# Group 0's root mean square as columns spread by a product, and its last two units normalised on ScalarE

## The chip, the cores and the metric

The kernel runs on one core of a Trainium2 chip. The metric is the device time of one execution in microseconds (us); lower is better. Instructions are carried out by TensorE (PE; its weight loads are shown as PEld), VectorE (DVE), ScalarE (ACT) and GpSimd (POOL), each in the order of its own queue; SyncE (SP) issues the transfers.

## The reference

Causal attention over 4 batches, 12 heads, 448 positions and a head width of 64, then a gated feed-forward layer on the 1792 tokens (model width 768, inner width 1536) with an RMS normalisation ahead of it:

```python
scores = np.where(mask, -1e9, q @ k.T / sqrt(64))
attn = softmax(scores)                      # sum + 1e-9 in the denominator
x = (attn @ v)  -> (1792, 768)
rms = np.sqrt(np.mean(x * x, axis=-1, keepdims=True) + 1e-06)
xn = x / rms * rms_g
g = xn @ w_gate
out = (g * sigmoid(g) * (xn @ w_val)) @ w_out
```

The weights come in as 64-bit numbers; the kernel turns them into 32-bit ones by integer steps.

## The kernel before

Attention is cut into 60 units (two heads and a block of queries each), in three groups: units 0 to 11 are group 0, 12 to 23 group 1, the rest group 2. A pair of units of group 0 makes one chunk `xr[0, c]` of 128 features by 512 tokens; there are six chunks, c = 0 to 5, and units 10 and 11 make the last one. A unit goes through scores (L192), mask and maximum (L201, VectorE), exponentials (L204, ScalarE), the reciprocal of the row sums (L213) and the multiplication with it (L207 on ScalarE for group 1, L209 on GpSimd for the others), transposes on TensorE (L249) with a copy of each half to `pt` (L253 VectorE, L255 ScalarE), products with the values (L275), and a copy to `xr` (L290).

Of each chunk `square` (L297) takes the squares; for group 0 GpSimd does this and the running sum `acc` for chunks 0 to 4 (both are shown as L103), and VectorE the square of chunk 5 (L308). `split_x` makes a rounded part `xh` (L328, ScalarE) and the rest `xl` (L329, VectorE). `rms` (L333) sums the squares over the features by products with a matrix of ones, so that each of the 128 rows of the result holds all 512 sums (L337), takes the root on ScalarE (L339) and four reciprocals of 128x128 on VectorE (L342). The result, `rinv[0]`, is multiplied into the first products by `evict` (L457).

The feed-forward layer walks over 36 weight chunks s (each 128x768) for a group. In the first pass a chunk is loaded (L360), converted (L379 ScalarE, L380 GpSimd, L382 and L384 VectorE), written back for later passes (L386), and split into `w_h` (L394, ScalarE) and `w_l` (L396, VectorE). Of `w_h` and `w_l` there are four buffers each, so that the cast of chunk 4 waits for TensorE's last use of chunk 0. Products are in triples (L440, L441, L442), six triples to a chunk; in what follows one triple is a part. The parts of weight chunks 0 to 2 with the chunks c of group 0 that are ready are done early, between the last units. The gate's products go through L457, a Tanh (L458), L459; the value's are multiplied in by L467; the product of both is rounded (L468) and its rest taken (L470).

The order of the work is written out by hand: a list of steps is walked, a slot number `now` goes up by one after each, and `post(delay, fn)` puts work into the slot `delay` later. Delays stand in the table `T`. Around the end of group 0 the slots are: 67 and 73 the multiplications of units 10 and 11; 75 the square and sum of chunk 4; 85 the products of unit 11; 87 the square of chunk 5, then the last part of token chunk 3; 88 `rms`; 88 to 90 the three parts of token chunk 4; 93 the conversion of weight chunk 5 (`CONVERT`, L47); from 94 the main loop with the parts of token chunk 5; 97 the cast of weight chunk 4; 98 the first `evict`.

```python
            if ENDS[0] <= p < ENDS[1]:
                pr["norms"].append(lambda: nc.scalar.mul(sp, sp, rs))
```

`ENDS` is (12, 24, 60), so p there is a unit of group 1. A later function, `x_steps` (L491), does for group 2 what the change does for group 0: sums as columns (L501), root (L503), reciprocal (L504), diagonal blocks (L510 on ScalarE, L512 on GpSimd), and a product that spreads them (L517).

Of the kernel before, what the change touches and what calls it, by code (L numbers as in the profile page):

```python
# [10 lines left out]
F32 = mybir.dt.float32  # L11
# [9 lines left out]
DM = H * D  # L21
# [17 lines left out]
        for g in range(NG) for c in range(NP)}  # L39
# [2 lines left out]


T = dict(c0=0, c1=1, c2=4, c20=12, c3=4, c30=13, c26=6, c36=7, c5=6, c50=16, c56=9, exp=1, exp0=3, gt=1, hh=1, hl=4, ws=5, ld2=7,
         ld=4, ld1=11, lv=5, norm0=7, norm1=2, r0=1, r1=5, so=3, wl=2, wl0=7, wl2=5, wl4=0, xl=2, xl0=9)
LOAD = (4, 12, 24, 36, 48, 60, 74, 86)
CONVERT = (20, 32, 44, 56, 62, 93)  # L47
SPLIT = (33, 45, 57, 70)
# [14 lines left out]
def attention_ffn(ctx: ExitStack, tc: tile.TileContext, qk0, qk1, qk2, v, v2, w, g, out, out2):  # L63
# [30 lines left out]
    def bank(tag, bufs=1):  # L94


        return ps.tile([P, W], F32, tag=tag, name=tag + "_ps", bufs=bufs)
# [23 lines left out]
    eps = const.tile([P, 1], F32, name="eps")  # L121
    nc.vector.memset(eps, 1e-6)
    tiny = const.tile([P, 1], F32, name="tiny")
    nc.vector.memset(tiny, 1e-9)
    g_sb = const.tile([P, KD], F32, name="g_sb")

# [4 lines left out]
    def post(delay, fn):  # L131
        if delay <= 0:
            fn()
        else:
            later.setdefault(now[0] + delay, []).append(fn)
# [36 lines left out]
    def steps_s(p):  # L172
# [22 lines left out]
        def softmax(e, i, pss):  # L195
            o, wd = bl[i]
            ps, sp = pss[e][:, o: o + wd], pr["sp"][e][:, o: o + wd]
            n = len(bl) * e + i
            nm, sm, rs = (pr[m][:, n: n + 1] for m in ("nm", "sm", "rs"))
            mk = mask2 if kind == 2 else mask[:, 3 * P - wd:]  # L200
            nc.vector.tensor_tensor_reduce(  # L201
                out=sp, in0=ps, in1=mk, scale=nsc, scalar=3.0e38,
                op0=ALU.add, op1=ALU.min, accum_out=nm)
            post(T["exp" if p >= ENDS[0] else "exp0"], lambda: nc.scalar.activation(  # L204
                sp, sp, AF.Exp, bias=nm, scale=-1.0, accum_out=sm))
            if ENDS[0] <= p < ENDS[1]:
                pr["norms"].append(lambda: nc.scalar.mul(sp, sp, rs))  # L207
            else:
                pr["norms"].append(lambda: nc.gpsimd.tensor_scalar(  # L209
                    sp, sp, rs, 1.0, op0=ALU.mult, op1=ALU.mult))  # L210
# [48 lines left out]
    def steps_a(p):  # L259


        if not 0 <= p < len(UNITS):
            return []
        g_, kind, c, k, _, base = UNITS[p]
        pr = hs[p]
        kb, nq = KB[kind], QUERIES[kind]

        def products():
            for h in range(1 + (kind == 2)):
                at = 0  # L270
                for j in range(NKB[kind]):
                    q0, n = ((0, 2 * P), (P, P))[j] if kind == 0 else (D * h, (P, D)[kind - 1])
                    a0 = at + (D * h if kind == 2 else 0)
                    for e in (0, 1):
                        nc.tensor.matmul(  # L275
                            av_ps[e * D: (e + 1) * D, p % 2, q0: q0 + n], raw_v[p][:kb, h, j, e, :],
                            pr["pt", e][:kb, a0: a0 + n], start=(j == 0), stop=(j == NKB[kind] - 1))
                    at += n if kind == 0 else P

        def copy():  # L280
            if g_ == 2 and base == 0:
                if c < 3:
                    xq[c] = w64_p.tile([P, 2, XT], F32, tag="w64", name="xq")
                xr[g_, c] = xq[c % 3][:, c // 3]
            elif base == 0:
                xr[g_, c] = xr_p.tile([P, W], F32, tag="xr", name="xr")
            x = xr[g_, c][:, base: base + nq]
            if p == LAST[g_, c]:
                post(2, lambda: square(g_, c))
            (nc.scalar.copy if g_ == 1 else nc.vector.tensor_copy)(x, av_ps[:, p % 2, :nq])  # L290

        return [products, copy]
# [4 lines left out]
    def square(b, c):  # L297

        halves = [(0, HX), (HX, XT)] if b == 2 else [(0, W)]
        for j, (lo, hi) in enumerate(halves):  # L300
            x = xr[b, c][:, lo: hi]
            sq = rm_p.tile([P, W], F32, tag="sq", name="sq") if c else \
                rm_p.tile([P, W], F32, tag="acc", name="acc", bufs=2)
            sq = sq[:, : hi - lo]
            if b:
                nc.scalar.activation(sq, x, AF.Square)
            elif c == NP - 1:
                nc.vector.tensor_tensor(sq, x, x, op=ALU.mult)  # L308
            else:
                pool_op(sq, x, ALU.mult, x)  # L310
            if c == 0:
                acc[b, j] = sq
            elif b or c < NP - 1:
                pool_op(acc[b, j], acc[b, j], ALU.add, sq)
        if b == 2:
            return
        if c == NP - 1:
            post(T["r1" if b else "r0"], lambda: rms(b, [acc[b, 0]] if b else [acc[b, 0], sq]))
        waiting.append((b, c))

    def split_x():
        if not waiting:
# [6 lines left out]
        post(T["xl0" if b == 0 and c < NP - 1 else "xl"], lambda: nc.vector.scalar_tensor_tensor(  # L329
            out=l, in0=x, scalar=gc, in1=f32(h), op0=ALU.mult, op1=ALU.subtract))  # L330
        xh[b, c], xl[b, c] = h, l

    def rms(b, parts):  # L333

# [688 lines left out]
```

## Time and profile before

| | us |
|---|---|
| median of 3 runs | 692.46 |
| lowest, highest | 692.16, 692.47 |
| the profiled execution | 691.53 |
| its span, first to last instruction | 689.8 |
| TensorE busy in the span | 669.2 (97%) |
| VectorE busy | 537.5 (78%) |
| ScalarE busy | 375.2 (54%) |
| GpSimd busy | 312.3 (45%) |

TensorE's granted clock was 1.000 of full speed over the span. The shares are means over stages with different limits; the wait that ends last in a stage tells more. In a timeline each line gives the start and the duration in us, the engine, the line of the kernel, the operation, output and inputs, and how many such instructions the line sums up; a bracket at its end tells how long the engine stood idle before it and what ended that. An instruction's duration can include time in which it stood at the head of its engine, unable to go on.

### The profile page before, as it was taken

What the parts mean: (1) busy time and instruction counts of PE and PEld (TensorE: products, weight loads), DVE (VectorE), ACT (ScalarE), POOL (GpSimd) and SP (SyncE); (2) the same over time, 40 slices, a digit from 0 to 9 for tenths busy, and PEclk for the clock granted to TensorE, in tenths of its full rate; (3) what the DMA queues carried; (4) which work ended last, traced back from release to release, by engine and by line L of the source; (5) the groups of instructions that cost most, each with busy time, mean ns of one, the idle gap of its engine ahead of it and who ended that gap; (6) DMA issues with size and microseconds to landing.
All of it is one profiled execution on the core that took longest, in us unless ns stands there. A gap on an engine that the chain in (4) does not pass through costs nothing. (4 is left out here: it accounts for less than half of the span.)

```text
span 689.8 us, 11922 instructions
## 1 busy us (share of the span) xinstructions
PE 669.2 (97%) x4108; PEld 548.8 (80%) x4108; DVE 537.5 (78%) x1048; ACT 375.2 (54%) x844; POOL 312.3 (45%) x281
## 2 busy tenths in 40 slices
PE   9889989999999999999999999999999999999997
PEld 6556767777776767777877777888999999999997
DVE  4996989899988577777686968389386768679993
ACT  6974577887887446345364544434434342455550
POOL 4994212131225533747666566663363536312220
PEclk9999999999999999999999999999999999999999
DMA  8663778788879646575757555324667576552541
GB/s 268 220 217 128 229 240 271 217 264 264 261 225 341 228 120 222 184 253 181 262 172 272 178 198 180 126 89 153 191 206 246 181 244 214 184 168 74 173 140 66
DMA packets 71356, 138.80 MB, mean 201 GB/s; under 512 B 7744, under 2 KB 39232, under 8 KB 71296
## 3 DMA queue, kind: packets, MB, share of 16 engines
q1 hardware_dynamic: 71296, 138.05, 62.1%
q8 instruction: 32, 0.52, 0.3%
q14 instruction: 28, 0.23, 0.1%
HBM read 104.21 MB, written 33.82 MB: 200 GB/s over the span
## 5 line engine op out<-in xcount | busy, mean ns | idle before, releaser
L209 POOL TENSOR_SCALAR sp<-sp,rs 128x128 f32<-128x128 f32 (+2 forms) x120 | 82.2, 704 | 89.5 <-DVE rs L213 84.7
L440 PE MATMUL m_ps<-xh,w_h 128*128 128x512 f32 x276 | 117.6, 426 | 4.0 <-DVE t_sb L467 3.0
L204 ACT ACTIVATE sp<-sp,nm 128x384 f32<-128x384 f32 (+3 forms) x168 | 87.1, 521 | 39.7 <-DVE nm L201 39.7
L442 PE MATMUL m_ps<-xh,w_l 128*128 128x512 f32 x276 | 108.5, 393 | 0.0
L441 PE MATMUL m_ps<-xl,w_h 128*128 128x512 f32 x276 | 108.2, 392 | 0.0
L380 POOL TENSOR_SCALAR w<-w 128x768 f32<-128x768 f32 x36 | 40.1, 1113 | 101.6 <-ACT w_c L379 93.5
L103 POOL TENSOR_TENSOR a_l<-w_q,a_h 128x768 fp32r<-128x768 f32 x24 | 47.1, 1964 | 66.6 <-ACT a_h L481 66.5
L275 PEld LDWEIGHTS a_ps<-pt,v_r 128*64 128x64 f32 (+1 forms) x864 | 41.7, 137 | 35.8 <-DVE pt L253 10.3
L275 PE MATMUL a_ps<-pt,v_r 128*64 128x128 f32 (+2 forms) x864 | 60.6, 268 | 7.6 <-DVE pt L253 5.6
L440 PEld LDWEIGHTS m_ps<-xh,w_h 128*128 128x128 f32 x276 | 51.9, 188 | 16.9 <-issue 7.5
L103 POOL TENSOR_TENSOR w_l<-w_r,w_h 128x768 fp32r<-128x768 f32 x30 | 59.5, 1990 | 7.3 <-ACT w_h L394 7.1
L442 PEld LDWEIGHTS m_ps<-xh,w_l 128*128 128x128 f32 x276 | 51.8, 188 | 11.8
L253 DVE COPY pt<-t_ps 128x384 f32<-128x384 f32 (+1 forms) x71 | 42.4, 598 | 23.7 <-PE t_ps L249 23.3
L201 DVE CUSTOM_DVE_ANT_0 sp<-s_ps,mask 128x128 f32<-128x128 f32 (+3 forms) x136 | 49.7, 414 | 12.2 <-PE s_ps L192 11.2
L440 PE MATMUL m_ps<-hh,w_h 128*128 128x512 f32 x144 | 58.6, 407 | 0.0
L441 PEld LDWEIGHTS m_ps<-xl,w_h 128*128 128x128 f32 x276 | 52.2, 189 | 7.8 <-issue 0.2
L442 PE MATMUL m_ps<-hh,w_l 128*128 128x512 f32 x144 | 56.3, 391 | 0.0
L441 PE MATMUL m_ps<-hl,w_h 128*128 128x512 f32 x144 | 56.2, 390 | 0.0
L249 PE MATMUL t_ps<-ident,sp 128*128 128x128 f32 (+1 forms) x309 | 50.3, 275 | 0.4 <-POOL sp L209 0.2
L249 PEld LDWEIGHTS t_ps<-ident,sp 128*128 128x128 f32 (+1 forms) x309 | 38.0, 138 | 14.9 <-POOL sp L209 2.2
L396 DVE TENSOR_TENSOR w_l<-w_c,w_h 128x768 fp32r<-128x768 f32 x36 | 40.1, 1114 | 4.3 <-ACT w_h L394 4.3
L384 DVE SCALAR_TENSOR_TENSOR w_c<-w_c,w 128x768 int32<-128x768 int32 x36 | 41.5, 1153 | 2.0
(185 smaller groups left out, 1677.8 us busy)
## 6 DMA issues: line engine op xcount, KB each, us to landing
w<-in_w SPq DMA_DIRECT2D x36, 768.0 KB, 5.2
w<-w_c SPq DMA_DIRECT2D x36, 384.0 KB, 5.8
w_r<-w SPq DMA_DIRECT2D x36, 384.0 KB, 4.8
qk_r<-in_qk SPq DMA_DIRECT2D x48, 256.0 KB, 4.2
qk_r<-in_qk SPq DMA_DIRECT2D x12, 512.0 KB, 5.7
v_r<-in_v SPq DMA_DIRECT2D x12, 448.0 KB, 4.7
v_r<-in_v SPq DMA_DIRECT2D x24, 192.0 KB, 3.1
wy<-w_r SPq DMA_DIRECT2D x24, 192.0 KB, 4.8
```

Of the source, the lines that this page charges most:

```text
L103: nc.gpsimd.tensor_tensor(out_, a, b, op=op)
L201: nc.vector.tensor_tensor_reduce(out=sp, in0=ps, in1=mk, scale=nsc, scalar=3.0e38, op0=ALU.add, op1=ALU.min, accum_out=nm)
L204: post(T["exp" if p >= ENDS[0] else "exp0"], lambda: nc.scalar.activation(sp, sp, AF.Exp, bias=nm, scale=-1.0, accum_out=sm))
L209: pr["norms"].append(lambda: nc.gpsimd.tensor_scalar(sp, sp, rs, 1.0, op0=ALU.mult, op1=ALU.mult))
L249: nc.tensor.transpose(ps[:kb, at: at + P], pr["sp"][e][:, o + kb * j: o + kb * (j + 1)], ident)
L253: nc.vector.tensor_copy(pt[:kb, :at], ps[:kb, :at])
L275: nc.tensor.matmul(av_ps[e * D: (e + 1) * D, p % 2, q0: q0 + n], raw_v[p][:kb, h, j, e, :], pr["pt", e][:kb, a0: a0 + n], start=(j == 0), ...
L380: (T["c1"], lambda: nc.gpsimd.tensor_scalar(hf_, hf_, 0.0, 1.0, op0=ALU.mult, op1=ALU.mult)),
L384: (at3, lambda: nc.vector.scalar_tensor_tensor(out=ti, in0=ti, scalar=3, in1=lo, op0=ALU.logical_shift_left, op1=ALU.bitwise_or)),
L440: nc.tensor.matmul(ps, wh[:, k, :], mh, start=(first and k == ks[0]), stop=False)
L441: nc.tensor.matmul(ps, wh[:, k, :], ml, start=False, stop=False)
L442: nc.tensor.matmul(ps, wl[:, k, :], mh, start=False, stop=(last and k == 5))
```

## The change

In group 0 the sums of squares are taken with the squares as stationary operand and one column of ones, so that the sum of each token lies in a row: four products for the sum of chunks 0 to 4 in slot 87, four for chunk 5 in slot 88. The root is then taken of 128x4 values. In slot 89 VectorE takes their reciprocal and multiplies the unit matrix with each of the four columns, which gives `dg`, 128x512; in slot 91 a product of ones with `dg` spreads the values to all rows, and ScalarE copies the result to `rms`. A root of one column is put into ScalarE's queue in slot 80, so that the table for roots is loaded there. Units 10 and 11 are normalised on ScalarE.

```diff
--- before.py
+++ after.py
@@ -42,7 +42,7 @@
 
 
 T = dict(c0=0, c1=1, c2=4, c20=12, c3=4, c30=13, c26=6, c36=7, c5=6, c50=16, c56=9, exp=1, exp0=3, gt=1, hh=1, hl=4, ws=5, ld2=7,
-         ld=4, ld1=11, lv=5, norm0=7, norm1=2, r0=1, r1=5, so=3, wl=2, wl0=7, wl2=5, wl4=0, xl=2, xl0=9)
+         ld=4, ld1=11, lv=5, norm0=7, norm1=2, r0=1, dg=1, spread=3, r1=5, so=3, wl=2, wl0=7, wl2=5, wl4=0, xl=2, xl0=9)
 LOAD = (4, 12, 24, 36, 48, 60, 74, 86)
 CONVERT = (20, 32, 44, 56, 62, 93)
 SPLIT = (33, 45, 57, 70)
@@ -121,6 +121,7 @@
     eps = const.tile([P, 1], F32, name="eps")
     nc.vector.memset(eps, 1e-6)
     tiny = const.tile([P, 1], F32, name="tiny")
+    warm_up = const.tile([P, 1], F32, name="warm_up")
     nc.vector.memset(tiny, 1e-9)
     g_sb = const.tile([P, KD], F32, name="g_sb")
 
@@ -203,7 +204,7 @@
                 op0=ALU.add, op1=ALU.min, accum_out=nm)
             post(T["exp" if p >= ENDS[0] else "exp0"], lambda: nc.scalar.activation(
                 sp, sp, AF.Exp, bias=nm, scale=-1.0, accum_out=sm))
-            if ENDS[0] <= p < ENDS[1]:
+            if ENDS[0] - 2 <= p < ENDS[1]:
                 pr["norms"].append(lambda: nc.scalar.mul(sp, sp, rs))
             else:
                 pr["norms"].append(lambda: nc.gpsimd.tensor_scalar(
@@ -285,6 +286,8 @@
             elif base == 0:
                 xr[g_, c] = xr_p.tile([P, W], F32, tag="xr", name="xr")
             x = xr[g_, c][:, base: base + nq]
+            if p == ENDS[0] - 2:
+                post(1, lambda: nc.scalar.activation(warm_up, eps, AF.Sqrt))
             if p == LAST[g_, c]:
                 post(2, lambda: square(g_, c))
             (nc.scalar.copy if g_ == 1 else nc.vector.tensor_copy)(x, av_ps[:, p % 2, :nq])
@@ -314,8 +317,11 @@
                 pool_op(acc[b, j], acc[b, j], ALU.add, sq)
         if b == 2:
             return
-        if c == NP - 1:
-            post(T["r1" if b else "r0"], lambda: rms(b, [acc[b, 0]] if b else [acc[b, 0], sq]))
+        if c == NP - 1 and b:
+            post(T["r1"], lambda: rms(b, [acc[b, 0]]))
+        elif c == NP - 1:
+            cols = column_sums(acc[b, 0], None, True)
+            post(T["r0"], lambda: rms_first(column_sums(sq, cols, False)))
         waiting.append((b, c))
 
     def split_x():
@@ -329,6 +335,34 @@
         post(T["xl0" if b == 0 and c < NP - 1 else "xl"], lambda: nc.vector.scalar_tensor_tensor(
             out=l, in0=x, scalar=gc, in1=f32(h), op0=ALU.mult, op1=ALU.subtract))
         xh[b, c], xl[b, c] = h, l
+
+    def column_sums(sq, ps, first):
+
+        ps = bank("t")[:, : W // P] if first else ps
+        for i in range(W // P):
+            nc.tensor.matmul(ps[:, i: i + 1], sq[:, P * i: P * (i + 1)], ones[:, :1],
+                             start=first and i == 0, stop=not first, skip_group_check=True)
+        return ps
+
+    def rms_first(ps):
+
+        rc = st_p.tile([P, W // P], F32, name="rc", bufs=1)
+        dg = ht_p.tile([P, W], F32, tag="t", name="dg")
+        r = rinv[0] = rm_p.tile([P, W], F32, tag="rms", name="rms", bufs=2)
+        nc.scalar.activation(rc, ps, AF.Sqrt, bias=eps, scale=1.0 / DM)
+
+        def diagonal():
+            nc.vector.reciprocal(rc, rc)
+            for i in range(W // P):
+                nc.vector.tensor_scalar_mul(dg[:, P * i: P * (i + 1)], ident, rc[:, i: i + 1])
+
+        def spread():
+            ps = bank("t")
+            nc.tensor.matmul(ps, ones, dg, start=True, stop=True)
+            nc.scalar.copy(r, ps)
+
+        post(T["dg"], diagonal)
+        post(T["spread"], spread)
 
     def rms(b, parts):
```

## Rows read from the trace of the kernel before

**Rows 1.** Stretches: PE, PEld, DVE, ACT, POOL busy (instructions), clock, DMA share, GB/s.

```profile
75.00:100.00 25.00, 20.98 (x100) 15.66 (x100) 23.59 (x49) 16.83 (x42) 4.10 (x4) 1.00 0.86 259
...
110.00:120.00 10.00, 10.00 (x56) 7.65 (x55) 9.88 (x20) 6.76 (x16) 2.27 (x2) 1.00 0.86 281
```

**Rows 2.** Timeline of TensorE: two of its waits for other engines.

```profile
53.99 0.44 PE L249 MATMUL x_ps<-ident,sp 128*128 128x128 f32 x2 [1.05 <-POOL sp L209]
...
88.32 0.47 PE L440 MATMUL m_ps<-xh,w_h 128*128 128x512 f32 x1 [2.08 <-DVE t_sb L467]
```

**Rows 3.** Timeline of VectorE: the four reciprocals and what follows them.

```profile
63.04 3.39 DVE L342 RECIPROCAL rms<-rms 128x128 f32<-128x128 f32 x4 [1.37 <-ACT rms L339]
66.35 0.90 DVE L396 TENSOR_TENSOR w_l<-w_c,w_h 128x768 fp32r<-128x768 f32 x1
```

**Rows 4.** Timeline of ScalarE around the root of group 0.

```profile
60.91 1.28 ACT L339 ACT_TABLE_LOAD   x1
62.32 0.69 ACT L339 ACTIVATE rms<-t_ps,eps 128x512 f32<-128x512 f32 x1
62.91 0.87 ACT L379 ACTIVATE w_c<-w 128x768 f32<-128x768 f32 x1
64.86 0.84 ACT L394 CAST w_h<-w_c 128x768 fp32r<-128x768 f32 x1 [1.08 <-PE m_ps L441]
```

**Rows 5.** Timeline of TensorE: the sums, then parts of token chunks 4 and 5.

```profile
60.40 1.02 PE L337 MATMUL t_ps<-acc,ones 128*128 128x512 f32 x2
...
62.81 0.40 PE L440 MATMUL m_ps<-xh,w_h 128*128 128x512 f32 x1
...
64.20 0.39 PE L440 MATMUL m_ps<-xh,w_h 128*128 128x512 f32 x1
```

**Rows 6.** Timelines of GpSimd, then VectorE, while units 10 and 11 are made.

```profile
46.28 1.87 POOL L103 TENSOR_TENSOR acc<-acc,sq 128x512 f32<-128x512 f32 x1
...
49.69 5.86 POOL L209 TENSOR_SCALAR sp<-sp,rs 128x128 f32<-128x128 f32 x8
...
51.98 1.96 POOL L209 TENSOR_SCALAR sp<-sp,rs 128x256 f32<-128x256 f32 x1
...
55.51 1.04 POOL L103 TENSOR_TENSOR sq<-xr 128x512 f32<-128x512 f32 x1
...
47.06 1.91 DVE L384 SCALAR_TENSOR_TENSOR w_c<-w_c,w 128x768 int32<-128x768 int32 x1
...
51.79 1.01 DVE L384 SCALAR_TENSOR_TENSOR w_c<-w_c,w 128x768 int32<-128x768 int32 x1
52.73 0.94 DVE L396 TENSOR_TENSOR w_l<-w_c,w_h 128x768 fp32r<-128x768 f32 x1
54.47 0.56 DVE L253 COPY pt<-x_ps 128x384 f32<-128x384 f32 x1 [0.79 <-PE x_ps L249]
```

**Rows 7.** Timelines of GpSimd and VectorE: a later running sum beside VectorE.

```profile
217.52 1.97 POOL L103 TENSOR_TENSOR acc<-acc,sq 128x512 f32<-128x512 f32 x1
...
218.28 1.76 DVE L329 SCALAR_TENSOR_TENSOR xl<-xr,g_sb,xh 128x512 fp32r<-128x512 f32 x1
```

**Rows 8.** Timeline of ScalarE: four multiplications of group 1; two copies of group 0.

```profile
86.76 1.49 ACT L207 ACTIVATE sp<-sp,rs 128x128 f32<-128x128 f32 x4 [2.83 <-DVE rs L213]
...
51.48 0.48 ACT L255 COPY pt<-t_ps 128x384 f32<-128x384 f32 x1 [1.65 <-PE t_ps L249]
...
56.46 0.48 ACT L255 COPY pt<-t_ps 128x384 f32<-128x384 f32 x1 [3.87 <-PE t_ps L249]
```

**Rows 9.** Timelines of TensorE, ScalarE, GpSimd: column sums, root and diagonal of group 2.

```profile
438.99 1.39 PE L501 MATMUL t_ps<-ones,acc 128*128 128x1 f32 x12
440.24 0.49 PE L440 MATMUL m_ps<-hh,w_h 128*128 128x512 f32 x1
...
440.42 0.27 ACT L503 ACTIVATE rc<-t_ps,eps 128x6 f32<-128x6 f32 x1 [2.38 <-PE t_ps L501]
...
441.08 1.60 POOL L512 TENSOR_SCALAR dg<-ident,rc 128x128 f32<-128x128 f32 x3 [0.94 <-DVE rc L504]
```

## The prediction

> **What bounds the kernel now.** I read the stretches first, because a share over the whole span hides them. From 110 us TensorE is busy in every microsecond; between 75 and 100 us it works 20.98 of 25 us while VectorE works 23.59 [rows 1]. So the reader is to see two stages: a long one in which only TensorE's own work or a late hand-over counts, and before it a short one, from the end of group 0's attention to about 106 us, in which VectorE is full and TensorE waits for it (the largest of these waits is 2.08 us, for the product of the two halves, L467 [rows 2]). All of this change lies in or just before that short stage. VectorE works its queue in order and stands still nowhere for long between 66.35 us and that wait; its few gaps are round trips of its own results through ScalarE. Hence one number decides: when does VectorE start the queue at the weight remainder `w_l` of chunk 4 (L396)? Before, at 66.35 us, right behind the four reciprocals of 3.39 us that began at 63.04 [rows 3]. Its other input, the cast `w_h`, was started at 64.86 [rows 4] and so done at 65.70; the reciprocals were the later one by 0.65 us. Every tenth by which this start moves, moves the TensorE wait at 88.32 and then the end, since behind 106 us nothing stands open that could take it up.
>
> Second, what comes before: the last two units (10 and 11) are normalised on GpSimd in eight multiplications, 5.86 us from 49.69; the last of unit 10 ended at 53.94, and TensorE waited 1.05 us for it [rows 2, 6].
>
> **The change part by part: the normalisation.** GpSimd loses the eight multiplications. ScalarE does four such in 1.49 us [rows 8], so it gets 2.98 us. Unit 10's are queued ahead of unit 11's exponentials, unit 11's behind the cast of chunk 3; ScalarE had 1.65 us idle before its copy at 51.48 [rows 8] and a little more ahead of that cast, so that copy of unit 10's transposes comes some 0.8 us later, at about 52.4. TensorE's 1.05 us wait goes. If nothing else moved, the next late thing would be VectorE's copy of the other half (L253): it needs VectorE free, which was so at 53.67, behind `w_l` (52.73 plus 0.94), where it now starts at 54.47 [rows 6]. Gain then: 0.8 us.
>
> But GpSimd's queue closes up. The square and the running sum of token chunk 4 stood behind the eight multiplications and ran at 55.51, when VectorE had little to do [rows 6]. With GpSimd free from 49.69 the square waits only for `xr`, whose copy stands in VectorE's queue right ahead of the conversion of chunk 4, and so it lands in that conversion: a first step (L382) that ends at about 51.7, just ahead of L384, then L384, then L396. These two engines shut each other out: the sum at 46.28 took 1.87 us, and L384 at 47.06, issued behind it, took 1.91 and ended 0.82 us after the sum did [rows 6]. So: square from 51.7, 1.04 us alone [rows 6] less 0.17 of start-up, to 52.6; L384 to 53.4; then the sum, issued at 52.6, 1.1 us (47.06 to 48.15 [rows 6]) to 54.5; L396 0.82 more, to 55.3; and only then the copy, 0.8 us later than before. TensorE's products of unit 10, and everything of group 0's end behind them, come 0.8 us late in place of 0.8 us early. I take this sum.
>
> Does the sum or L396 come first at 53.4? Two rows differ. The sum issued at 217.52 went ahead of a VectorE operation issued at 218.28, which ended 0.55 us after it [rows 7]; but the multiplication issued at 51.98 ended only at 53.94, behind L396, which was issued later, at 52.73, and ran its undisturbed 0.94 us [rows 6]. That multiplication carries a per-token factor and the sum does not, so I go by rows 7. The Trainium skill, page "SBUF — State Buffer", section "Who interferes with whom", has one rule for it: "Issue order, not op shape, decides who blocks". By that rule the sum goes first, as in my forecast; the multiplication at 51.98 doesn't follow it, and by that row the result would be the second rival below.
>
> **The table load.** It took 1.28 us at 60.91 and was over by 62.32, when the last product came in [rows 4], so moving it saves nothing by itself. It moves ahead of ScalarE's copy of unit 11's transposes, before which ScalarE had 3.87 us idle [rows 8]: hidden there. Without that cover the new, shorter chain would show up to 1.3 us of it.
>
> **The sums on TensorE.** Removed: four passes of 512 columns, from 60.40 to 62.81 less one part (one triple of products, 0.69 us: 62.81 to 64.20 is two), so 1.72 us [rows 5]. Added: eight products of one column, two instructions each; twelve such instructions took 1.25 us, 438.99 to 440.24 [rows 9], so two lots of eight are 1.67 us; and the spread, half of what was removed, 0.86 us. In all 0.8 us more on TensorE, of which the first lot stands ahead of the part of chunk 3 and the spread behind the three parts of chunk 4. The spread thus starts at 60.40 + 0.8 (late) + 1.67 + 2.08 = 64.95. Its operand: the columns are in at about 62.9, the square root is 0.27 us [rows 9], the reciprocal of four columns less, and four multiplications of 128x128 on VectorE, which the trace doesn't show. On ScalarE one is 0.37 us at most (a mean with wider ones [rows 8]), on GpSimd 0.53 [rows 9]: with the first they end at 64.9, just in time; with the second 0.6 us late, which TensorE would wait. Anything cheaper changes nothing. I take no wait, the first row being nearer to VectorE's kind, and keep 0.6 for the upper end. `dg` takes one of four rotating `t` buffers and gives it back before the second evict needs it: nothing.
>
> **The reciprocals and the copy.** VectorE is rid of 3.39 us [rows 3] and gets some 1.5. That would be the gain, but what is late next takes it. The spread's result is copied to `rms` on ScalarE, and this copy is put into its queue at slot 91. Behind it there stand the conversion of chunk 5 (L379, slot 93) and the cast `w_h` of chunk 4 (L394, slot 97); before, they ran at 62.91 and 64.86, the second waiting for TensorE alone [rows 4]. Now both wait behind a copy that waits for the spread. Two instructions of the old product ran 1.02 us to the end of the second [rows 5]: the spread ends at 65.97, the copy starts at 66.0, takes 0.6 (62.32 to 62.91 of the square root, as wide [rows 4]), L379 0.8 to 0.87, L394 0.84 [rows 4]: the cast is done at 68.25. VectorE waits for it with `w_l`, and behind `w_l` stand the first gate product and all of the full stage. Start at 68.25 in place of 66.35: 1.9 us later. VectorE's saving of 1.9 us turns into idle time ahead of it.
>
> **The sum.** +1.9 us, carried to the end. The profiled execution, 691.53 us (its span of 689.8 and 1.73 around it, which stay), becomes 693.4; the median of the runs is 0.93 above the profiled execution, so 692.46 + 1.9 = 694.4 us. Differences under about 0.2% (1.4 us) can't be told from none here.
>
> **Rivals.** (a) *GpSimd does not get in the way*: the square and the sum lose to VectorE each time. Then group 0 ends 0.8 us early, the spread starts at 63.35, the cast is done at 66.65: +0.3, 692.8 us, not slower by anything measurable. It is decided at the end of the conversion before L384: against it, 47.06 [rows 6]. Chance 0.1. (b) *Half of it*: the square goes ahead of L384, the sum behind L396, as the multiplication at 51.98 did. The copy then starts at 54.2, 0.3 early; spread at 63.85, cast at 67.15: +0.8, 693.3 us. Chance 0.2. (c) *The saved VectorE time arrives*: ScalarE's queue is not the bound, either because the copy comes early enough or because the casts stand ahead of it. Then the first cast is bound by the part of chunk 0 behind the spread, which frees its buffer; with (a) that is 63.35 + 0.86 + 0.65, cast done at 65.7: -0.65, 691.8 us; more would need the full stage itself to close up, for which I see one sort of reason, other encounters of GpSimd and VectorE behind 66 us. Against it: the slots, by which the copy precedes both. Chance 0.12, half of it faster by more than 0.2%. (d) *The operand of the spread is late* by 0.6: 695.0 us, chance 0.15. The forecast as it stands has 0.43.
>
> **How the numbers follow.** Slower by more than 0.2% (over 693.85 us): the forecast and (d), and a little of (b), 0.62. Within 0.2%: (a), most of (b), half of (c), 0.32. Faster: 0.06. The range reaches down past (a) to 692.2, and up past (d) to 695.3; the forecast's own range is 693.9 to 694.9.
>
> **What would show it.** Right: GpSimd's square near 51 us with some 1.7 us and its sum to about 54.5; L384 and L396 of that place stretched to 1.6 and 2.0 us; the copy L253 at 55.2; the spread at about 64.9 with no wait; ScalarE's copy near 66, then L379 and L394 without a pause; VectorE idle up to a `w_l` at 68.2; TensorE's waits of 1.05 and 2.08 us still there, 1.9 us later. Wrong: the copy L253 at 53.7 to 54.2 (rivals a, b), a `w_l` before 66.4 (c), a wait of TensorE at the spread for VectorE (d). If the late start shows but the TensorE wait at 88 us shrinks by as much, my claim that nothing behind takes it up was wrong.

## The result, and the profile after

The changed kernel takes 700.36 us (median of 4 runs, 699.13 to 700.65), the kernel before 692.31 beside it (4 runs, 690.93 to 692.47): a ratio of 1.0117, with a 95% interval from 1.0100 to 1.0135. It is 8.05 us slower; 694.4 was forecast, and the upper end of the range was 695.3. The profiled execution of after took 700.35 us, with a span of 698.6 against 689.8.

Laying VectorE's rows of the two traces side by side shows where the 8.8 us come in. After is 0.64 late from its first softmax on (the first load landed that much later; this differs from one execution to the next and is not the change's). It is 2.47 late at `w_l` of chunk 4, 2.4 to 2.9 late all through the long stage up to 490 us, and then 8.5 late at 514. So there are two places: the one that the prediction is about, worth 1.83, and another at the start of the last stage, 420 us later, worth 6.

The first place. Timelines of after, GpSimd, VectorE, TensorE, ScalarE and again VectorE (start us, us, engine, line, operation, tiles, count, idle before and what ended it; lines of after are numbered higher: L418 is L384 of before, L430 L396, L254 L253, L413 L379, L428 L394):

```profile
51.56 1.61 POOL L103 TENSOR_TENSOR sq<-xr 128x512 f32<-128x512 f32 x1 [1.25 <-DVE xr L293]
53.26 1.86 POOL L103 TENSOR_TENSOR acc<-acc,sq 128x512 f32<-128x512 f32 x1
...
52.32 1.68 DVE L418 SCALAR_TENSOR_TENSOR w_c<-w_c,w 128x768 int32<-128x768 int32 x1
53.92 2.02 DVE L430 TENSOR_TENSOR w_l<-w_c,w_h 128x768 fp32r<-128x768 f32 x1
55.85 0.55 DVE L254 COPY pt<-x_ps 128x384 f32<-128x384 f32 x1
...
65.63 1.02 PE L361 MATMUL t_ps<-dg,ones 128*128 128x512 f32 x2
...
66.69 0.59 ACT L362 COPY rms<-t_ps 128x512 f32<-128x512 f32 x1 [2.79 <-PE t_ps L361]
67.17 0.90 ACT L413 ACTIVATE w_c<-w 128x768 f32<-128x768 f32 x1
67.96 0.82 ACT L428 CAST w_h<-w_c 128x768 fp32r<-128x768 f32 x1
...
68.82 1.03 DVE L430 TENSOR_TENSOR w_l<-w_c,w_h 128x768 fp32r<-128x768 f32 x1 [3.80 <-ACT w_h L428]
```

The reader is to see the chain of the prediction, link by link: GpSimd's square and sum lie in VectorE's conversion and stretch L418 and L430 to 1.68 and 2.02 (before: 1.01 and 0.94, [rows 6]); the copy L254 is late; the spread starts without a wait; ScalarE's copy waits 2.79 for it, with L413 and the cast behind; and VectorE stands 3.80 for the cast, where before it came straight from the reciprocals [rows 3].

What the prediction has no word of is TensorE's clock. In two stretches of after it was granted half of full speed (the lower of its two levels, 1.2 GHz) all or most of the time; in the trace of before it is 1.00 in both:

```profile
52.00:54.00 2.00, 2.00 (x7) 1.41 (x6) 1.97 (x3) 1.98 (x5) 1.92 (x2) 0.50 0.92 337
...
92.00:94.00 2.00, 2.00 (x11) 1.06 (x9) 0.99 (x2) 1.97 (x7) 0.00 (x0) 0.53 0.86 213
```

(The columns are those of [rows 1]; the clock is the third from the end.) Neither costs anything in this trace. The first lies ahead of TensorE's wait for the copy L254, which is the shorter for it; the second follows a wait of 2.10 us at 90.93, where VectorE is full, and VectorE is as late at 105 us as at 85 (2.62).

The second place. After's timelines of SyncE, ScalarE, TensorE and VectorE where the last stage begins:

```profile
490.99 0.43 SPq L487 DMA_DIRECT2D out_t<-ob  x1
...
494.58 0.48 ACT L647 COPY m<-m_ps 128x384 f32<-128x384 f32 x1 [4.81 <-DMA out_t<-ob]
...
495.11 0.69 PE L624 MATMUL m_ps<-ch,a_h 128*128 128x384 f32 x1 [2.58 <-ACT m L647]
495.60 0.52 PE L624 MATMUL m_ps<-cl,a_h 128*128 128x384 f32 x1
...
498.58 0.34 PE L624 MATMUL s_ps<-ch,a_l 128*128 128x384 f32 x1
...
514.41 0.96 DVE L684 TENSOR_TENSOR wq<-wq 128x768 f32<-128x768 f32 x1 [2.86 <-DMA wq<-w]
...
515.89 0.45 PE L624 MATMUL y_ps<-ch,a_h 128*128 128x384 f32 x1 [1.89 <-DVE c L658]
```

And the same place before, on ScalarE and VectorE:

```profile
488.39 0.48 ACT L613 COPY m<-m_ps 128x384 f32<-128x384 f32 x1 [1.25 <-PE m_ps L590]
...
491.94 0.55 DVE L618 TENSOR_TENSOR u<-m,s_ps 128x384 f32<-128x384 f32 x1 [3.97 <-DMA out_t<-ob]
```

`ob` is the last result of group 1; its store is issued at 490.99. The results of the last stage, `m` and `u` among them, lie in a pool (`hs`) that is opened where the pools of the feed-forward part have been closed, in the memory that these give back; what takes the place of `ob` has to wait for its store. Before, the store is waited for as well, but by VectorE's `u` (L618), which nobody needs yet: TensorE does not stop. After, it is waited for by ScalarE's copy of the very first product of the last stage, `m`. That copy frees a PSUM bank; TensorE wants it and stands 2.58 us. The stretches 490 to 495 and 495 to 500, first of before, then of after (busy us of PE, PEld, DVE, ACT, POOL with instructions, TensorE's granted clock, share and GB/s of the transfers):

```profile
490.00:495.00 5.00, 5.00 (x31) 5.00 (x30) 2.72 (x5) 2.85 (x4) 3.59 (x2) 1.00 0.56 176
495.00:500.00 5.00, 5.00 (x31) 5.00 (x30) 2.82 (x7) 2.13 (x5) 0.08 (x1) 1.00 0.56 159
```

```profile
490.00:495.00 5.00, 2.53 (x15) 2.21 (x13) 0.60 (x2) 0.42 (x2) 0.00 (x0) 0.99 0.53 178
495.00:500.00 5.00, 4.89 (x20) 4.89 (x21) 3.07 (x4) 4.02 (x6) 2.13 (x2) 0.67 0.23 67
```

Behind this idle the granted clock falls, to a mean of 0.67 over 495 to 500 (0.50 at 496 to 498): the matmuls there start 0.32 apart instead of 0.175, nine of them, 1.3 us more. Later VectorE is held by the weights `wq`, whose transfer now lands late, and TensorE stands 1.89 at 515.89, where it stood 0.25 before. Waits of 2.58 and 1.64 more, and 1.3 for the clock, are 5.5 of the 6 us that come in between 490 and 516. The 1.64 need not be the store's doing: from the first issue of `wq` to VectorE's start it is 8.7 us in after and 7.1 in before, and in the other traces of this study anything from 6.1 (e2) to 8.5 (e15). The one tile of the change that could shift the place of `ob` is `dg`, which is drawn from the same rotating tiles.

### The profile page after: what moved, and what is told of

The parts are those of the page before. It is cut to its first block, busy times and chain, and to the rows that moved or that the text cites. A ratio compares the mean times of both kernels' runs of the same rounds, so it can differ in the third digit from the quotient of the medians.

```text
span 698.6 us, 11946 instructions
## 1 busy us (share of the span) xinstructions
PE 674.9 (97%) x4122; PEld 553.7 (79%) x4122; DVE 538.6 (77%) x1049; ACT 378.0 (54%) x854; POOL 307.8 (44%) x273
## 5 line engine op out<-in xcount | busy, mean ns | idle before, releaser
L210 POOL TENSOR_SCALAR sp<-sp,rs 128x384 f32<-128x384 f32 (+2 forms) x112 | 76.2, 697 | 90.4 <-DVE rs L214 85.6
L254 DVE COPY pt<-t_ps 128x384 f32<-128x384 f32 (+1 forms) x71 | 42.5, 598 | 23.9 <-PE t_ps L250 23.5
L430 DVE TENSOR_TENSOR w_l<-w_c,w_h 128x768 fp32r<-128x768 f32 x36 | 41.4, 1149 | 8.1 <-ACT w_h L428 8.1
L193 PE MATMUL s_ps<-qk_r 64*128 64x128 f32 (+3 forms) x296 | 43.6, 432 | 0.5 <-DVE nm L202 0.4
```

What stands on the lines that cost most here:

```text
L193: nc.tensor.matmul(ps, r[:, q0: q0 + nq], r[:, k0: k0 + wd], start=True, stop=True)
L210: pr["norms"].append(lambda: nc.gpsimd.tensor_scalar(sp, sp, rs, 1.0, op0=ALU.mult, op1=ALU.mult))
L254: nc.vector.tensor_copy(pt[:kb, :at], ps[:kb, :at])
```

## The experiments

Times are medians; each kernel is compared with runs of the kernel before on the same chip (691.92, 691.93, 691.48 and 691.74 in the four sessions). "`w_l`" is the start of chunk 4's remainder in the profiled execution (66.35 before). Executions start up to 0.6 us apart, so "late" is how much later than before it comes, less how much later VectorE's copy to `xr` at 42.44 came, which is ahead of all that the changes touch.

| kernel | us (lowest to highest, runs) | ratio to before, interval | `w_l` | late |
|---|---|---|---|---|
| the change | 700.36 (699.13 to 700.65, 4) | 1.0117, 1.0100 to 1.0135 | 68.82 | 1.8 |
| e1_dg_apart | 695.07 (694.52 to 695.96, 4) | 1.0051, 1.0036 to 1.0066 | 70.02 | 3.3 |
| e2_before_pad1 | 695.32 (692.92 to 695.69, 5) | 1.0044, 1.0028 to 1.0060 | 66.65 | 0.0 |
| e3_before_pad4 | 693.42 (691.46 to 695.01, 10) | 1.0022, 1.0010 to 1.0034 | 66.63 | 0.0 |
| e9_before_norms_scalar | 693.91 (692.61 to 696.52, 6) | 1.0035, 1.0018 to 1.0051 | 68.52 | 2.3 |
| e4_norms_gpsimd | 693.53 (692.34 to 694.28, 10) | 1.0022, 1.0012 to 1.0032 | 67.24 | 1.1 |
| e7_squares_later | 696.33 (694.92 to 697.70, 4) | 1.0062, 1.0040 to 1.0085 | 69.85 | 3.4 |
| e11_idle_filled | 694.74 (694.05 to 695.70, 4) | 1.0052, 1.0037 to 1.0067 | 68.42 | 1.9 |
| e5_copy_vector | 694.88 (693.12 to 697.28, 10) | 1.0046, 1.0031 to 1.0061 | 68.30 | 1.4 |
| e8_all | 696.20 (694.02 to 696.77, 7) | 1.0052, 1.0036 to 1.0067 | 69.93 | 3.6 |
| e10_square_scalar | 693.45 (691.86 to 698.46, 10) | 1.0045, 1.0020 to 1.0069 | 67.17 | 1.0 |
| e12_square_scalar_copy | 693.96 (691.46 to 698.34, 10) | 1.0041, 1.0018 to 1.0063 | 70.32 | 3.4 |
| e14_wide_sums | 693.37 (691.48 to 694.90, 10) | 1.0020, 1.0009 to 1.0032 | 67.53 | 0.6 |
| e15_rms_alone_wide | 693.78 (692.14 to 696.45, 10) | 1.0029, 1.0015 to 1.0042 | 67.08 | 0.7 |
| e13_before_both_scalar | 691.98 (690.62 to 692.77, 10) | 1.0007, 0.9998 to 1.0017 | 66.59 | -0.2 |

**Is it the place of the last `ob`?** Only `dg`'s place is changed, from one of the four rotating tiles to the tile of the squares:

```diff
-        dg = ht_p.tile([P, W], F32, tag="t", name="dg")
+        dg = rm_p.tile([P, W], F32, tag="sq", name="dg")
```

> The changed kernel, with dg in the single buffer of the squares (rm_p, tag sq) in place of one of the four rotating t buffers; all else as changed. Theory A (rotation): dg moves every later t buffer of the feed-forward part on by one, so the last ob of group 1 lies where the copy m (m1) of the last stage is written, ScalarE waits 4.81 us for its store at 489 us, TensorE 2.58 us for ScalarE; with dg elsewhere this goes, the late start of w_l (about 1.9 us) stays: 694 us (693.4 to 694.6), and the copy m starts within 1.5 us of its product. Theory B (lag): the store is late because the whole program runs 2.5 us later than the loads it shares SyncE with; then dg's place changes nothing: 700 us, and ScalarE still waits over 4 us for the store.

695.07: 5.3 us back for one line, if not quite down to my 694.6. ScalarE's copy `m` waits for its product again and VectorE's `u` for the store, as before; TensorE's clock stays up in the last stage. Theory B is out: at 485 us this execution is 3.9 later than before, more than after's 2.6, and `m` does not wait for the store.

```profile
492.31 0.48 ACT L647 COPY m<-m_ps 128x384 f32<-128x384 f32 x1 [1.23 <-PE m_ps L624]
...
495.69 0.56 DVE L652 TENSOR_TENSOR u<-m,s_ps 128x384 f32<-128x384 f32 x1 [3.79 <-DMA out_t<-ob]
...
490.00:495.00 5.00, 5.00 (x30) 4.88 (x29) 1.16 (x2) 3.18 (x5) 1.84 (x2) 1.00 0.79 264
```

The other way round: the kernel before, with nothing of the change, only one more rotating tile drawn at the place of `dg` (and then four):

```diff
     def rms(b, parts):
 
+        for _ in range(0 if b else 1):
+            spare = ht_p.tile([P, W], F32, tag="t", name="spare")
+            nc.gpsimd.memset(spare[:, :1], 0.0)
```

> The kernel before, with one t buffer taken and one column of it set by GpSimd at the root of group 0, and nothing else. Theory A (rotation): +6 us, 698 to 699 us, with ScalarE's copy m waiting for the store of the last ob and no change before 480 us. Theory B (lag): no change, 692.3 us.

One spare tile costs 3.4 us in the median (695.32); theory A had 6. The profiled execution, the quickest of the five and only 1.0 above before, shows the same wait as after, and TensorE's idle without the fall of the clock; what the other four have more, no trace shows:

```profile
491.55 0.48 ACT L616 COPY m<-m_ps 128x384 f32<-128x384 f32 x1 [4.04 <-DMA out_t<-ob]
...
492.08 0.44 PE L593 MATMUL m_ps<-ch,a_h 128*128 128x384 f32 x1 [1.79 <-ACT m L616]
```

> The kernel before, with four t buffers taken in the same place, one whole turn of the four. Theory A (rotation): back in place, 692.3 us (within 0.5), VectorE's u waiting some 4 us for the store as in the kernel before. If it is any extra allocation or instruction that costs, not the place in the turn: 698 us or more. Theory B: 692.3 as well.

Four spare tiles do not come back to the kernel before, as theory A had it: 693.42. No one waits for the store of `ob` any more, so it lies in a third place, and the tiles are not a strict turn of four; which one a request gets I did not work out. The 1.5 us have another cause: ScalarE's table load for the first gate now stands behind a wait for `gr`, and the gate's Tanh with it; VectorE is 1.3 later behind it.

```profile
490.00 0.48 ACT L616 COPY m<-m_ps 128x384 f32<-128x384 f32 x1 [1.25 <-PE m_ps L593]
...
491.62 0.55 DVE L621 TENSOR_TENSOR u<-m,s_ps 128x384 f32<-128x384 f32 x1 [2.05 <-ACT a_h L484]
...
68.20 1.28 ACT L461 ACT_TABLE_LOAD   x1 [2.23 <-DVE gr L460]
```

So one tile more or less drawn from this set, with hardly any work, decides who waits for the store in the last stage, and that costs microseconds: this holds in both directions (e1, e2). Not settled are the size, which in e2 is half of theory A's, and the order in which the tiles are given out (e3).

**The two halves of the change.** The normalisation on ScalarE alone, in the kernel before (rms in its old form):

```diff
-            if ENDS[0] <= p < ENDS[1]:
+            if ENDS[0] - 2 <= p < ENDS[1]:
```

> The kernel before, with only units 10 and 11 normalised on ScalarE. My theory (GpSimd's square and sum of token chunk 4 close up and hold VectorE's conversion): the copy of the last half of unit 10 starts 0.8 us later than before, reciprocals and w_l follow 0.8 us later: 693.1 us (692.8 to 693.4). Rival (the normalisation brings what it removes, TensorE's 1.05 us wait): 691.5 us.

693.91, above my 693.4: slower by itself, in spite of the TensorE wait of 1.05 that it removes. The row of L396 shows the encounter with GpSimd (2.01 for 0.94), the next one what it costs: TensorE waits 2.73 for the late copy. The stretch 54 to 56 is all but empty, and 58 to 60, behind it, has a granted clock of 0.52. The copy L253 is 0.8 late, as forecast; the half clock adds 1.5, since from this copy to the next one it is 5.25 us, where before has 3.72.

```profile
53.18 2.01 DVE L396 TENSOR_TENSOR w_l<-w_c,w_h 128x768 fp32r<-128x768 f32 x1
...
55.72 0.86 PE L275 MATMUL a_ps<-pt,v_r 128*64 128x256 f32 x6 [2.73 <-DVE pt L253]
...
54.00:56.00 2.00, 0.28 (x4) 0.21 (x5) 1.66 (x2) 0.00 (x0) 0.38 (x1) 1.00 1.03 317
58.00:60.00 2.00, 2.00 (x7) 1.44 (x6) 0.00 (x0) 0.00 (x0) 0.00 (x0) 0.52 0.18 64
```

The column form alone (e1 with that line as it was before):

> The changed kernel with the diagonal's tile apart (695.07 in the earlier run, +3.15 on the kernel before) and the last two units normalised on GpSimd again, so only the column form of the rms is left. Mine: the norms' half of the change was forecast at about +1 and then let TensorE idle 2.7 us at 53 to 56 us and run at half clock after it; without it the copies of L254 come back early, TensorE waits under 1.5 us there, its granted clock stays at 1.0 in 56 to 62, and w_l of slot 13 stands 0.5 to 1.5 later than in the kernel before: 692.8 to 693.6. Rival: the column form alone costs it (the chain root, reciprocal, diagonals, spread, copy), the norms nothing: then it stays at 694.5 to 695.5 with w_l 2.5 or more later.

693.53, within what was expected; L430 takes its 0.94 again, and `w_l` is 1.1 late, VectorE waiting for the cast in ScalarE's queue:

```profile
52.52 0.94 DVE L430 TENSOR_TENSOR w_l<-w_c,w_h 128x768 fp32r<-128x768 f32 x1
...
67.24 1.02 DVE L430 TENSOR_TENSOR w_l<-w_c,w_h 128x768 fp32r<-128x768 f32 x1 [3.73 <-ACT w_h L428]
```

Neither half gains anything: alone they are slower by 2.0 and 1.6 us.

**Can GpSimd be got out of the way?** First by a later issue of the square (e1 with it):

```diff
-            else:
+            elif c < NP - 2:
                 pool_op(sq, x, ALU.mult, x)
...
+            elif not b and c == NP - 2:
+                def late(sq=sq, x=x):
+                    pool_op(sq, x, ALU.mult, x)
+                    pool_op(acc[0, 0], acc[0, 0], ALU.add, sq)
+                post(6, late)
```

> The changed kernel with the diagonal's tile apart (695.07), and the square and sum of the last-but-one chunk put six slots later on GpSimd. Mine: GpSimd's multiplications no longer stand against VectorE's L418, L430 and L254 at 51 to 56 us, the copy L254 that TensorE waits for at 56.2 comes back some 2 us earlier, TensorE's idle of 2.72 us falls under 1.5, its granted clock stays at 1.0 in 56 to 62, and w_l goes from +3.67 to about +1: 692.2 to 693.0. Rival: the encounter only moves to where the square now stands (one more of 1 to 2 us between 56 and 62, under the sums of columns): 694.5 to 695.5.

A miss, and of my own making: GpSimd has nothing else queued there, so a later issue leaves its queue in the very same order, and it starts the square as soon as `xr` is there:

```profile
51.02 1.61 POOL L103 TENSOR_TENSOR sq<-xr 128x512 f32<-128x512 f32 x1 [1.25 <-DVE xr L293]
```

It is therefore e1 once more, on another chip, and tells how far one program varies: the eight executions of the two lie between 694.52 and 697.70, median 695.57. Then by giving that square to ScalarE, with column sums of its own:

```diff
+            fifth = b == 0 and c == NP - 2
...
-            if b:
+            if b or fifth:
                 nc.scalar.activation(sq, x, AF.Square)
...
+            if fifth:
+                acc[0, 4] = sq
...
             cols = column_sums(acc[b, 0], None, True)
+            column_sums(acc[0, 4], cols, False)
```

> The changed kernel with the diagonal's tile apart (695.07), and the square of the last-but-one chunk taken from GpSimd and made by ScalarE (its sums of columns are four more small products into the same accumulation, no sum by GpSimd). Mine: GpSimd has nothing to do between 50 and 60 us, so VectorE's L418 and L430 take 1.0 and 0.95 instead of 1.68 and 2.0, the copy L254 comes 1.7 earlier, TensorE idles 1.0 there instead of 2.72, its granted clock stays at 1.0 in 56 to 62, and w_l of the last slot goes from +3.67 to between 0 and +0.7: 691.8 to 692.8. Rival: ScalarE's square (0.7) stands ahead of its copies L256 and of xh, and TensorE idles for these instead: 693.8 to 695.5.

Now the encounter is gone, and with it 2.4 us of `w_l` (3.3 late to 1.0 late), TensorE's idle (0.94 instead of 2.72) and the fall of the clock. The median is 693.45, lower than e1's (their intervals overlap) but above my 692.8, and the executions spread from 691.86 to 698.46. VectorE's rows of that place:

```profile
51.58 0.96 DVE L422 SCALAR_TENSOR_TENSOR w_c<-w_c,w 128x768 int32<-128x768 int32 x1
52.45 0.95 DVE L434 TENSOR_TENSOR w_l<-w_c,w_h 128x768 fp32r<-128x768 f32 x1
53.32 0.55 DVE L254 COPY pt<-x_ps 128x384 f32<-128x384 f32 x1
...
67.17 1.02 DVE L434 TENSOR_TENSOR w_l<-w_c,w_h 128x768 fp32r<-128x768 f32 x1 [3.69 <-ACT w_h L432]
```

**Is it the idle that takes the clock?** e1, with TensorE's idle filled by five products that nothing reads:

```diff
                     for e in (0, 1):
+                        if p == ENDS[0] - 2 and j == 0 and e:
+                            for _ in range(5):
+                                nc.tensor.matmul(
+                                    av_ps[e * D: (e + 1) * D, p % 2, q0: q0 + n], raw_v[p][:kb, h, j, e, :],
+                                    pr["pt", 0][:kb, a0: a0 + n], start=True, stop=True)
```

> The changed kernel with the diagonal's tile apart (695.07), with five more matmuls of 128x256 ahead of the product that waits for VectorE's copy at 53.5 to 56.2 us (they write where that product then writes; nothing reads them). Mine: the idle is what takes TensorE's clock; with 1.5 to 2.2 of its 2.7 us filled the granted clock stays at 1.0 in 56 to 62, the matmuls after it take 0.39 instead of 0.63, and w_l of the last slot comes 1.2 to 1.7 earlier than without them: 693.3 to 694.0. Rival: the clock falls for another reason, and nothing is gained, or the added matmuls cost their own time: 695 to 697.

The stretches 54 to 56 and 58 to 60 of e1, then of this kernel, and its `w_l`:

```profile
54.00:56.00 2.00, 0.00 (x0) 0.00 (x0) 2.00 (x2) 0.77 (x2) 0.84 (x1) 1.00 0.74 244
...
58.00:60.00 2.00, 2.00 (x6) 1.41 (x6) 0.00 (x0) 0.05 (x1) 0.00 (x0) 0.50 0.40 145
```

```profile
54.00:56.00 2.00, 1.06 (x5) 0.41 (x3) 2.00 (x2) 0.63 (x2) 0.73 (x1) 1.00 0.78 254
...
58.00:60.00 2.00, 1.93 (x12) 1.09 (x11) 0.83 (x2) 0.00 (x0) 0.00 (x0) 1.00 0.30 112
...
68.42 1.03 DVE L435 TENSOR_TENSOR w_l<-w_c,w_h 128x768 fp32r<-128x768 f32 x1 [3.71 <-ACT w_h L433]
```

With products that do nothing the clock stays up and `w_l` comes 1.5 us earlier (1.9 late for 3.3), as I expected of the idle. The time does not follow: the median of 694.74 misses my 693.3 to 694.0, and set against the kernel before on its own chip it is 1.0052, where e1 is 1.0051 and e7 1.0062. So the idle's part in the clock is shown in the traces; that keeping the clock up is worth 1.5 us of the time is not shown.

**ScalarE's queue, and the rest.** The copy of rms on VectorE, first in e1:

```diff
-            nc.scalar.copy(r, ps)
+            nc.vector.tensor_copy(r, ps)
```

> The changed kernel with the diagonal's tile apart (695.07), and rms copied out of PSUM by VectorE instead of ScalarE. Mine: the copy stands on ScalarE ahead of L413 (0.59 us) and w_h (L428) behind it, which w_l waits for; w_l comes 0.5 to 0.8 earlier, 694.2 to 694.6. Rival: VectorE's queue ahead of the copy takes it up, or ScalarE's next waits are others: 695.0 within 0.3.

694.88, the rival's figure. `w_l` comes 0.5 earlier than in after (68.30 for 68.82; both executions started 0.6 late), but the time does not. Two other waits take over: the cast now stands 2.78 for TensorE's use of chunk 0, and the four diagonals take 1.50 instead of 0.88, beside GpSimd's conversion, which no longer stands behind the copy and runs at 64.74. Then the copy, e7's edit, and the spread one slot earlier:

> The three together (diagonal's tile apart, last-but-one square later, copy of rms by VectorE) and the spread one slot earlier. Mine: the gains add: 691.2 to 692.0, so at or a little under the kernel before (691.9). Rival: the spread, a slot earlier, waits on TensorE for the diagonals (0.5 to 1.0 us, all units behind it): 692.5 to 693.5.

A miss: 696.20. e7's edit does nothing (above), and the spread, as the rival said, waits 0.78 for the diagonals with all of TensorE behind it:

```profile
66.77 1.10 PE L366 MATMUL t_ps<-dg,ones 128*128 128x512 f32 x2 [0.78 <-DVE dg L362]
```

And the copy in e10:

> The kernel with the last-but-one square on ScalarE, and rms copied out of PSUM by VectorE. Mine: w_h of the last slot stands 0.6 earlier on ScalarE, w_l with it: 691.2 to 692.2, at or below the kernel before (691.9). Rival: as without the copy's move, within 0.3.

693.96, 2.5 above before, from 691.46 to 698.34; my 691.2 to 692.2 is missed. Its profiled execution was one of the long ones (696.05), and shows where: TensorE's sums of one column, sixteen instructions and then eight, the parts of chunk 4 behind them, and the stretches 60 to 62 and 62 to 64.

```profile
59.16 1.95 PE L347 MATMUL t_ps<-ones,acc 128*128 128x1 f32 x16
...
61.76 1.70 PE L347 MATMUL t_ps<-ones,sq 128*128 128x1 f32 x8
63.32 0.77 PE L478 MATMUL m_ps<-xh,w_h 128*128 128x512 f32 x1
63.89 0.63 PE L479 MATMUL m_ps<-xl,w_h 128*128 128x512 f32 x1
...
60.00:62.00 2.00, 2.00 (x15) 1.86 (x16) 1.17 (x2) 0.45 (x1) 0.00 (x0) 0.93 0.03 9
62.00:64.00 2.00, 2.00 (x9) 1.90 (x10) 0.18 (x1) 0.50 (x2) 0.00 (x0) 0.50 0.00 0
```

The clock falls at 61.7 and is back at 68.6, and the rows have TensorE busy nearly all the time from 54.65 on; but for 1.95 us of it it had made sums of one column. Do the long executions come from there? The same sums with 128 columns of ones, the same operands:

```diff
-        ps = bank("t")[:, : W // P] if first else ps
+        ps = bank("t") if first else ps
         for i in range(W // P):
-            nc.tensor.matmul(ps[:, i: i + 1], sq[:, P * i: P * (i + 1)], ones[:, :1],
+            nc.tensor.matmul(ps[:, P * i: P * (i + 1)], sq[:, P * i: P * (i + 1)], ones,
...
-        nc.scalar.activation(rc, ps, AF.Sqrt, bias=eps, scale=1.0 / DM)
+        nc.scalar.activation(rc, ps[:, ::P], AF.Sqrt, bias=eps, scale=1.0 / DM)
```

> The kernel with the last-but-one square on ScalarE and the copy of rms on VectorE (693.96, executions from 691.46 to 698.34), its sums of columns made with 128 columns of ones instead of one (same operands, same sums, 128 times written). Mine: TensorE's granted clock fell at 61.9 us in the profiled execution of that kernel behind products of one column, with no idle before; with 128 columns it stays at 1.0, no execution lies above 694.5, and the median is 691.5 to 692.5. Rival: the long executions come from elsewhere (the idle of 1 us before, the transfers, the last stage): the spread stays at 691.5 to 698 with a median over 693.3.

The long executions are gone: at most 694.90 (I had 694.5), where e10 and e12 have seven of twenty above 696. The clock holds in the profiled one:

```profile
59.13 2.05 PE L347 MATMUL t_ps<-ones,acc 128*128 128x128 f32 x16
...
62.00:64.00 2.00, 2.00 (x13) 1.74 (x13) 0.77 (x4) 1.05 (x2) 0.05 (x1) 1.00 0.00 0
```

But the median, 693.37, stays above what I expected, and the column form alone with these sums gains nothing on e4 either:

> The column form of rms alone (diagonal's tile apart, norms on GpSimd as in the kernel before; 693.53 with sums of one column and ScalarE's copy), with sums of 128 columns and rms copied by VectorE. Mine: the copy gives 0.6 of w_l back, the clock stays: 692.0 to 693.0, so no gain over the kernel before (691.5 to 691.9). Rival: the one-column products alone made it slow: 691.0 to 691.8.

693.78, above my 693.0, with one execution of ten at 696.45. So the sums of one column are a possible cause of the long executions in e10 and e12, not a shown one: only one of these was traced, e4 has such sums and no execution above 694.28, and e15 has none and one of 696.45. They are not why the column form is slower.

Last, the kernel before with norms and that square on ScalarE, and rms in its old form, by three products instead of two:

> The kernel before with units 10 and 11 normalised by ScalarE (693.91 in the earlier run) and the last-but-one square on ScalarE as well, rms in its old form with three products of 128x512 instead of two. Mine: nothing of GpSimd stands against VectorE, TensorE's wait of 1.05 for GpSimd's normalising is gone and its clock stays up; the third product costs 0.5 where TensorE is busy: 691.0 to 692.2. Rival: the old rms form's four reciprocals (3.39 us on VectorE) set w_l whatever comes ahead of them: 692.8 to 694.

691.98: no difference from the kernel before. The half of the change that moves the norms is free once GpSimd's square is moved too; it is no gain either, since the four reciprocals still set `w_l`:

```profile
63.29 3.39 DVE L345 RECIPROCAL rms<-rms 128x128 f32<-128x128 f32 x4 [2.22 <-ACT rms L342]
66.59 0.90 DVE L399 TENSOR_TENSOR w_l<-w_c,w_h 128x768 fp32r<-128x768 f32 x1
```

No kernel of the study beats the kernel before.

## Why the prediction was wrong

The direction held, and so did the chain of waits at the end of group 0 that it was built on; the size did not, because one term that the sum put at nothing was some 6 us, and because the sum had no term for TensorE's clock.

- **The encounter of GpSimd and VectorE: right.** Less its 0.64 of late start, after's square starts at 50.9 (forecast near 51), L418 and L430 take 1.68 and 2.02 (1.6 and 2.0), the copy L254 starts at 55.2 (55.2). The sum, issued at 53.26, went ahead of L430, issued at 53.92, which ended 0.82 after it: as in [rows 7], and as the Trainium skill's rule of issue order has it (page "SBUF — State Buffer", section "Who interferes with whom"). Rivals (a) and (b) fall with that row. (The 0.17 of start-up that the forecast takes off the square stands in no row; the square ended at 52.5 for the 52.6 forecast.)
- **The spread's operand: right.** Four diagonals take 0.88 on VectorE, TensorE does not wait; rival (d) is out. It was close: in e5 they took 1.50, and one slot earlier (e8) TensorE waited 0.78.
- **ScalarE's queue: right.** Copy at 66.05, `w_l` at 68.18 less the late start, forecast 66.0 and 68.2. VectorE's saved 1.9 us did become idle time; rival (c) is out. TensorE's wait of 1.05 at 53.99 [rows 2] is gone, as the prediction says of the normalisation, though its list of signs has a wait of 1.05 that stays (there is another one at 81.87 in before, 1.33 at 84.48 in after); one for VectorE of 1.14 takes its place. The wait of 2.08 at 88.32 is there, 2.10 at 90.93.
- **The step that failed: "`dg` takes one of four rotating `t` buffers and gives it back before the second evict needs it: nothing".** I asked who waits for `dg`, and stopped when no one did. The request also moves every later one of the same set, as far as the last `ob`, 420 us on, whose store the last stage must wait for. That is 6 us in the trace of after (1.6 of it the transfer of `wq`, which may not belong to it), 5.3 by e1, and by e2 3.4 in the median and 1.0 in the traced execution.
- **"Behind 106 us nothing stands open that could take it up"** was read only for gains. A wait of 3.97 us for the store stood in VectorE's queue at 491.94 in the trace of before: covered, but one engine away from TensorE. I had not looked at it. Nor is TensorE "busy in every microsecond" from 110 us on: that was read from ten of them, and before has seven waits behind, up to 0.78 at 546.04.
- **No price for TensorE's clock behind an idle.** The sum took the late copy as 0.8 us of delay. In after it was no more, since the clock had fallen and risen earlier (0.50 at 52 to 54), hidden; that 1.83 came so near the forecast 1.9 is luck of this execution. In e1, e7, e8 and e9 the idle of 2.7 us at that place was followed by some 3 us at half speed, 1.5 us more at `w_l` (3.3 late in e1). The Trainium skill (page "TensorE: Matmul & The Clock Gate", section "What's actually happening") says that the point at which the clock changes level differs from run to run of one kernel. After and e1, with the same TensorE work up to there, agree: 0.50 at 52 to 54 in the one, at 58 to 60 in the other.
- **Size of the group 0 end.** 1.9 forecast; over executions, e1 with e7 stands 3.65 above the kernel before. 1.83 of it is the forecast's chain in after's trace; the clock's 1.5 would be most of the rest, by the traces, but e11, where the clock stays up, is not quicker for it. The other 4.4 of the 8.05 (4.9 by e1 alone) goes with the place of `ob`.
- **Still open:** why the column form alone (e4, e15) is 1.6 to 2.0 us slower in the median with a `w_l` only 0.7 to 1.1 late. In the traced executions the rest comes in the last stage, and not at one place: in e15 TensorE's wait for `wq` is 1.70, where before has 0.25; in e4 there is none, but from 626 us on its matmuls of 128x384 start 0.177 us apart, where every other trace has 0.173, at a granted clock of 1.00 in both, and that is 1.1 us by the end. Neither is explained. And by what order the rotating tiles are given out (e3).

## What to carry to other kernels

A tile drawn from a shared rotating set is an edit to all that draws from that set later: list who draws next, down to the last transfer out of it, and look for a covered wait there that would move onto another engine. Taken from another set, the same tile cost nothing there (e1). An engine that gets rid of work starts its next work earlier, and what this meets has to be priced as well as what is saved. Where an edit makes TensorE idle, count the matmuls behind the idle at half speed as one case of the sum.

## What the runs showed of the hardware

TensorE's granted clock, 1.00 (the level of 2.4 GHz) in nearly every stretch, fell to 0.50 (1.2 GHz) for some 3 us behind idles of 2.6 to 2.7 us (after's last stage, e1, e7, e8, e9), and five products without use kept it up (e11). Behind the wait of 2.1 us near 90 us it fell in seven traces (after, e4, e9, e10, e11, e12, e15) and stayed up in eight (before, e1, e2, e5, e7, e8, e13, e14); VectorE is full there, and the fall made nothing later. An idle of 1.8 did not take it (e2). The idle alone does not tell: of 48 to 50 us TensorE worked 0.51 in before and 0.65 in after and in e12; the clock was 0.50 at 52 to 54 in after and stayed at 1.00 in the other two. It also fell once with TensorE busy, behind 1.95 us of matmuls of one column, for 6.8 us (e12); in e10's trace, with the same sums, and in e14's, with 128 columns, it did not. A matmul of 128 columns takes the same time as one of a single column, 2.05 us for the sixteen instructions in place of 1.95. A matmul of 128x512 took 0.63 at the low level and 0.39 at the high one.
